# Moving small work between ACT, VectorE and a PSUM bank in the attention part of a sparse-attention and mixture-of-experts kernel

## The chip, the cores and the metric

The kernel runs on one core of one Trainium2 chip. The metric is the device time of one launch in microseconds. The engines are named as in the profile: PE is TensorE (PEld its weight loads), DVE is VectorE, ACT is ScalarE, POOL is GpSimd, SP is SyncE, which issues most of the DMAs.

## What is computed

Attention over 8 batches, 8 heads, 576 positions and 64 channels a head, with two masks of stride 32: heads 0 to 3 look at the last 32 positions, heads 4 to 7 at positions with the same remainder modulo 32. Its output, 512 numbers a position, goes into a gated layer of 8 experts that picks one expert for each position:

```python
scores = scale * np.matmul(q, k.transpose(0, 1, 3, 2))
scores = np.where(masks[None, :, :, :], scores, -1000000000.0)
attn = softmax(scores)                       # over keys
x = (attn @ v) as (B, S, H * D)
...
logits = np.einsum('bsd,de->bse', x, w_gate)
local_gate = sigmoid(x @ w_local)
for b in range(B):
    prev_e = -1
    for s in range(S):
        fresh_e = int(np.argmax(logits[b, s]))
        e = fresh_e if s == 0 or local_gate[b, s] < 0.5 or prev_e < 0 else prev_e
        prev_e = e
        h = np.maximum(x[b, s] @ w1[e], 0.0)
        out[b, s] = softmax(logits[b, s])[e] * (h @ w2[e])
```

## The kernel before

**Two parts.** The first part (`attention`, 0 to about 164 us) computes attention, writes the rows x to memory (`xd`), computes logits and gates, and makes the list of rows for the first expert's first tiles. The second part (`Experts.run`) takes the experts in turn: rows are gathered by an indirect DMA, turned, multiplied by w1, passed through relu, multiplied by w2 and scattered to the output. Pairs of row tiles are multiplied with seven products of half matrices in place of eight, for which sums of the weights (`Weights.sums`, L729) are needed.

**Steps.** The first part is written out by hand, without a scheduler: each engine runs its instructions in the order in which the loop over `n` (L450) issues them. There are 32 pairs of heads, (batch, pair), four a batch, and step n works on several of them at once, as a pipeline:

- it loads operands for pair n + 4, and in steps 5 to 12 a piece of the first expert's weights (SP);
- it computes scores and exponentials of pair n (PE, then ACT; a mask on DVE for the first two pairs of a batch), in two units;
- it stores rows of pair n - 2 if a half batch is complete (`store_x`, POOL for batches 0 and 1, SP after them);
- it turns the rows of pair n - 2 (`turn_x`, L322: PE transposes into PSUM at L330, ACT copies to `xT` at L334);
- it multiplies the exponentials of pair n - 1 by the values (`values`, L288) and divides by the sums (`norm`, L301 and L302 on DVE), unit by unit;
- then, in this order: two pieces of the weight sums (L732 on DVE, in steps 10 to 17), the gates of a batch (`gates`, L372), the stores of probabilities (`store_p`, L411, POOL), the logits of a batch (`logits`, L343), and last what `also[n]` holds.

**Logits and gates.** With `last` the last pair of batch b, logits(b) is in step last + 2 = 4b + 5: steps 5, 9, 13, ... Its products (L354) go to the bank pair of `psT`; the products of the four blocks of channels land on four groups of 32 partitions, and a second product (L382, in `gates`) adds the four groups with a matrix of ones (`fold`). Between the two stands a copy from PSUM to `lT` in four parts: 504 columns and 72 columns of 64 partitions, twice, the second time with the columns in another order. Batches 1, 3 and 5 are twins (`TWINS`, L63) of the batch before: their logits are added to the same `lT` by DVE (L366), and the gates of both are computed together. So gates run for batches 0 and 1 in step 10, 2 and 3 in step 18, 4 and 5 in step 26, 6 in step 30, 7 in step 34. `gates` reads its product four times on DVE (L388, L391, L394, L396) and then works in SBUF.

**PSUM.** Three pools hold 8 banks: `psS` (scores, two buffers of two banks), `psT` (one buffer of two banks: turned rows, logits, and all that asks for `bank()`, L420), `psV` (two buffers of one bank: value products, one for each unit, and the gates). A buffer is given out in turn; its first writer waits until the readers of its last use are done.

**The first gather.** Steps 19 to 29 compute the list of rows (`router.steps` and `router.table`, put into `also`); its last function, `numbers` (L660), runs in step 29, and the index that the gather uses is written at L665. `moe.gather` (L763, L765 on POOL) fetches two tiles of rows, `moe.scale` (L771 on ACT) uses them in step 31.

Of the kernel before, what the change touches and what calls it, by code (L numbers as in the profile page):

```python
# [8 lines left out]
F32 = mybir.dt.float32  # L9
# [9 lines left out]
P = 128  # L19
B, H, S, DH = 8, 8, 576, 64  # L20
# [6 lines left out]
V1 = DH + 1  # L27
# [44 lines left out]
def spread(ap, shape):  # L72

    dims = list("abcd"[:len(shape) - 1])
    left = " ".join(dims[:-1] + [f"({dims[-1]} o)"])
    right = " ".join(dims + ["o"])
    return ap.rearrange(f"{left} -> {right}", o=1).to_broadcast(shape)
# [7 lines left out]
def across(ap, shape):  # L85

    return ap.rearrange("a (o b) -> a o b", o=1).to_broadcast(shape)
# [60 lines left out]
def attention(ctx, tc, qkl, qks, vl, vs, wg, xd, ident, router, moe):  # L148
# [11 lines left out]
    psV = ctx.enter_context(tc.tile_pool(name="psV", bufs=2, space=PSUM))  # L160
# [3 lines left out]
    def load(b, pair):  # L164
        local = pair < PAIRS // 2
        src = qkl if local else qks
        t = inp.tile([P, qkl.shape[-1]], F32, name="qk")
        st["qk", b, pair] = t
        nc.sync.dma_start(out=t[:, 0:src.shape[-1]], in_=src[b, pair % 2])
        if pair % 2 == (b == 0 and local):  # L170
            shape = [LK, LT, 4, V1] if local else [GK, GT, 4, V1]
            t = vals.tile(shape, F32, name="vl" if local else "vs")
            nc.sync.dma_start(out=t, in_=(vl if local else vs)[b])
            st["v", b, local] = t
# [6 lines left out]
    def busy(n):  # L181
        for _ in range(n):
            ps = psV.tile([P, 512], F32, name="vps")
            nc.tensor.matmul(ps, lhsT=warm[:, 0:P], rhs=warm, start=True, stop=True)
# [28 lines left out]
    for n, c in blocks:  # L213

        i, div = consts.tile([GK, 1], I32, name=f"row{n}"), consts.tile([GK, 1], F32, name=f"div{n}")
# [55 lines left out]
    def mask(u):  # L271
        if u.local:
            ev = u.e[:, :, 0:3 * LQ]
            m = maskL[:, 3 * u.g:3 * u.g + 3].rearrange("p a x -> p (a x)")
            nc.vector.tensor_tensor(ev, ev, m.rearrange("p (o x) -> p o x", o=1).to_broadcast([LK, 2, 3 * LQ]),
                                    op=Alu.mult)
# [66 lines left out]
    def logits(b):  # L343
        xT = st["xT", b]
        n = GK * (GT - 1)
        both = ((0, slice(0, n)), (1, slice(n, S)))
        final = b == B - 1

        second = b in TWINS
        w = slice(0, 32) if second else slice(16, 48)  # L350

        ps = [psS.tile([P, 2, 512], F32, name="sps") for _ in range(2)] if final else [psT.tile([P, 2, 512], F32, name="tps")] * 2
        for kk, a, c in [(kk, *x) for kk in range(DK) for x in both] if final else [(kk, *x) for x in both for kk in range(DK)]:
            nc.tensor.matmul(ps[kk // 2][32 * kk:32 * kk + 32, a, 0:c.stop - c.start], lhsT=wgs[:, kk, w], rhs=xT[:, kk, c],  # L354
                             start=True, stop=True, skip_group_check=True)
        if not second:
            st["lT", b] = small.tile([P, S], F32, name="lT")
        lT = st["lT", b] = st["lT", TWINS.get(b, b)]
        o = lT[64:].rearrange("p (y c) -> p y c", c=STRIDE)
        parts = [(lT[0:64, 0:n], ps[0][0:64, 0, 0:n]), (lT[0:64, n:], ps[0][0:64, 1, 0:GL]),  # L360
                 (o[:, :, 0:GC * (GT - 1)].rearrange("p y (j c) -> p j y c", c=GC),
                  ps[1][64:, 0, 0:n].rearrange("p (j y c) -> p j y c", j=GT - 1, c=GC)),
                 (o[:, :, GC * (GT - 1):], ps[1][64:, 1, 0:GL].rearrange("p (y c) -> p y c", c=GR))]
        for i, (to, of) in enumerate(parts):
            if second:
                nc.vector.tensor_tensor(to, of, to, op=Alu.add)  # L366
            elif i == (1 if final else 2) or i == 0:
                nc.scalar.copy(out=to, in_=of)
            else:
                nc.vector.tensor_copy(to, of)  # L370

    def gates(b):  # L372

        b0 = TWINS.get(b, b)
        n = b - b0 + 1
        ps = psV.tile([P, 2, 3, V1], F32, name="vps").rearrange("p a i e -> p (a i e)")
        lt = ps[:, 0:CH * n * (E + 1)].rearrange("p (t b e) -> p t b e", b=n, e=E + 1)
        to = fold.rearrange("p (b x) -> p b x", b=2)[:, 0:n, 0:E + 1]
        for t in range(CH):
            m = min(P, S - t * P)  # L380
            for o in range(0, P, m):
                nc.tensor.matmul(lt[o:o + m, t], lhsT=st["lT", b][:, t * P:t * P + m], rhs=to,  # L382
                                 start=(t == 0), stop=True, skip_group_check=True)
        lg = lt[:, :, :, 0:E]
        one, shape = [P, CH, n], [P, CH, n, E]
        f = lambda name, shape: small.tile(shape, F32, name=f"{name}{n}")
        mx = f("gmx", one)
        nc.vector.tensor_reduce(mx, lg, axis=AX.X, op=Alu.max)  # L388
        mxb = spread(mx, shape)
        ex = f("ex", shape)  # L390
        nc.vector.tensor_tensor(ex, lg, mxb, op=Alu.subtract)  # L391

        eq = f("eq", shape)
        nc.vector.tensor_tensor(eq, lg, mxb, op=Alu.is_equal)  # L394
        fr = f("fr", one)
        nc.vector.scalar_tensor_tensor(fr, lt[:, :, :, E], FRESH, spread(start, one), Alu.is_le, Alu.max)  # L396
        nc.scalar.activation(ex, ex, Act.Exp)
        flat = eq.rearrange("p t b e -> p (t b) e")
        nc.vector.tensor_tensor(flat, flat, across(down, [P, CH * n, E]), op=Alu.mult)
        code = f("code", one)  # L400
        nc.vector.tensor_reduce(code, eq, axis=AX.X, op=Alu.max)
        nc.vector.tensor_tensor(code, spread(pos8, one), code, op=Alu.subtract)

        nc.vector.tensor_tensor(codes[:, :, b0:b + 1], spread(code, shape), spread(fr, shape), op=Alu.mult)
        sm = f("gsm", one)
        nc.vector.tensor_reduce(sm, ex, axis=AX.X, op=Alu.add)
        nc.vector.tensor_scalar(sm, sm, 1e-9, None, Alu.add)
        nc.vector.reciprocal(out=sm, in_=sm)
        nc.vector.tensor_tensor(probs[:, :, b0:b + 1, 0:E], ex, spread(sm, shape), op=Alu.mult)
# [10 lines left out]
    def bank():  # L420
        return psT.tile([P, 8, P], F32, name="tps").rearrange("p a x -> p (a x)")
# [10 lines left out]
    also = {n: [] for n in range(len(units) + 3)}  # L432
# [7 lines left out]
    m = n  # L440
# [2 lines left out]
    early = router.table(0, bank, rooms)  # L443
    for i, do in enumerate(early):
        also[m + i].append(do)
    also[m + 5].append(lambda: moe.gather(moe.first))
    also[len(units) - 1] += [lambda: moe.scale(moe.first)]

    steps = []
    for n in range(len(units) + 3):  # L450
        if n < len(units):
            if n + ahead < len(order):
                load(*order[n + ahead])
            if 5 <= n < 13:
                moe.W[0].load(nc, moe.w1, moe.w2, 0, n - 5)
            if n == 10:
                steps = moe.W[0].sums(nc.vector)
            for u in units[n]:
                scores(u)
                mask(u)  # L460
        if 0 <= n - 2 < len(units) and order[n - 2][1] % 2 == 1:
            store_x(units[n - 2][1])
        if 0 <= n - 2 < len(units) and n != len(units):
            turn_x(*order[n - 2])
        if 0 <= n - 1 < len(units):
            for u in units[n - 1]:
                values(u)
                norm(u)
        if n == len(units):
            turn_x(*order[n - 2])  # L470
            moe.turn(moe.first, spare, 0)
        elif n == len(units) + 1:
            busy(FILL)
        for do in steps[:2]:
            do()
            steps.remove(do)
        for b in range(B):
            last = PAIRS * b + PAIRS - 1
            if n == last + 3 and b + 1 not in TWINS:
                gates(b)  # L480
            if n == last + 4 and b < B - 1 and b + 1 not in TWINS:
                for both in {TWINS.get(b, b), b}:
                    store_p(both)
            if n == last + 2:
                logits(b)
        if n == len(units) + 1:
            moe.turn(moe.first, bank, 1)
            busy(2)
            moe.row_sums(moe.first)
        for do in also[n]:  # L490
            do()
# [1056 lines left out]
```

## Time and profile before

| what | value |
|---|---|
| median of 3 runs | 684.21 us (683.5 to 684.27) |
| the profiled execution | 684.04 us |
| its span, first to last instruction | 682.3 us |
| mean granted clock of PE | 0.994 |
| PE busy | 662.7 us (97%) |
| PE busy in 0 to 164 us | 157.78 us |
| DVE, ACT, POOL busy in the span | 355.5, 194.2, 117.5 us |

The page gives busy time per engine, the granted clock of PE in 40 slices, and the chain of work that ended last. The list of waits says which engine stood idle before which line, until which line on which engine ended: "PE tps L330 <- DVE lT L366: 1.2, 2, 0.9" is 1.2 us in total in 2 places, 0.9 the longest. A line of the timeline has the start in us from the span's start, the duration of the group in us, engine, line, operation, output <- inputs, shape, count, and in brackets the idle time before it with what ended it. A line of the stretches has the stretch and its length, busy time and count for PE, PEld, DVE, ACT and POOL, the granted clock, the share of the DMA engines and GB/s.

### The profile page before, as it was taken

The page shows a single profiled execution, that of the slowest core. Times are in us where ns is not written, and L with a number is a line of the kernel's source. Part 1 is how long each engine was busy: PE and PEld are TensorE (multiplying, and loading weights), DVE is VectorE, ACT ScalarE, POOL GpSimd, SP SyncE. Part 2 cuts the span into 40 slices and gives each one's busy share as a digit, 9 for nine tenths or more (in the row PEclk, how much of TensorE's full clock was granted, in tenths as well). Part 3 has the DMA queues.
Part 4 walks back from the last instruction along what each step waited for, and adds up shares of the span by engine and source line. Part 5 has one row for each costly group of instructions (what it writes and reads, how often), then busy time and mean ns, then how long its engine had stood idle before and what let it go on. Part 6 is the DMA issues. An engine that isn't in the chain of part 4 may idle for free.

```text
span 682.3 us, 14753 instructions
## 1 busy us (share of the span) xinstructions
PE 662.7 (97%) x6020; PEld 570.5 (84%) x6020; DVE 355.5 (52%) x791; ACT 194.2 (28%) x356; POOL 117.5 (17%) x144
## 2 busy tenths in 40 slices
PE   9999999999999999999999999999999999999994
PEld 6888788777998999589979998997799899699493
DVE  6567867846894448026523664651256556522131
ACT  3545445343322221312222222121222232221220
POOL 3431010112021023012011202302111112121001
PEclk9999999989999999999999999999999999999998
DMA  9999877744410182081145217111712622021001
GB/s 324 405 373 331 283 276 276 258 117 140 177 60 35 35 291 69 24 290 36 48 150 174 64 46 268 52 32 40 259 40 65 238 71 73 34 56 42 18 9 37
DMA packets 35801, 95.84 MB, mean 140 GB/s; under 512 B 4790, under 2 KB 11702, under 8 KB 35628
## 3 DMA queue, kind: packets, MB, share of 16 engines
q1 hardware_dynamic: 27164, 71.41, 29.7%
q0 software_dynamic: 7936, 22.38, 10.4%
q8 instruction: 66, 1.08, 0.7%
q14 instruction: 107, 0.88, 0.4%
q10 hardware_dynamic: 528, 0.10, 0.1%
HBM read 74.69 MB, written 19.69 MB: 138 GB/s over the span
## 4 chain that ended last, share of the span: by engine, by line
PE 57%; issue 1%; DVE 1%; DMA 1%; ACT 0%; POOL 0%; POOLq 0%; ACTq 0%
PE lps L835 22%; PE mps L871 21%; PE mps L937 4%; PE lps L926 3%; PE mps L967 2%; PE lps L947 2%; PE xps L778 2%; DMA x<-xd,gi 1%; PE lps L957 0%; DVE h L958 0%; ACT y L973 0%; POOL out_dram L791 0%; DVE wt L732 0%; DVE y L823 0%; ACT x L771 0%
## 5 line engine op out<-in xcount | busy, mean ns | idle before, releaser
L791 POOL DMA_INDIRECT out_dram<-y,tab x40 | 46.1, 1154 | 352.6 <-DVE y L823 248.5
L835 PE MATMUL lps<-tt,ws 128*128 128x128 f32 x768 | 91.8, 275 | 0.6 <-issue 0.6
L835 PEld LDWEIGHTS lps<-tt,ws 128*128 128x128 f32 x768 | 88.6, 192 | 1.0 <-issue 0.8
L871 PE MATMUL mps<-wt,k 128*128 128x256 f32 x384 | 85.7, 380 | 0.0
L871 PEld LDWEIGHTS mps<-wt,k 128*128 128x128 f32 x384 | 72.8, 190 | 9.9
L835 PE MATMUL lps<-xt,w1t 128*128 128x128 f32 x512 | 63.2, 277 | 3.0 <-ACT y L973 1.9
L835 PEld LDWEIGHTS lps<-xt,w1t 128*128 128x128 f32 x512 | 60.4, 192 | 6.5 <-ACT y L973 3.7
L823 DVE TENSOR_TENSOR h<-lps,u 128x512 f32<-128x512 f32 x48 | 33.1, 690 | 57.5 <-PE lps L835 55.8
L871 PE MATMUL mps<-w2t,h 128*128 128x256 f32 x256 | 60.5, 379 | 0.0
L268 ACT ACTIVATE e<-sps 128x576 f32<-128x576 f32 (+1 forms) x64 | 41.5, 650 | 54.3 <-PE sps L264 53.3
L765 POOL DMA_INDIRECT x<-xd,gi x40 | 41.1, 1027 | 82.4 <-PE lps L835 26.3
L871 PEld LDWEIGHTS mps<-w2t,h 128*128 128x128 f32 x256 | 47.4, 190 | 5.8
L264 PE MATMUL sps<-qk 64*128 64x96 f32 (+2 forms) x704 | 51.2, 282 | 0.5 <-issue 0.4
L264 PEld LDWEIGHTS sps<-qk 64*128 64x128 f32 (+2 forms) x704 | 43.0, 185 | 8.8 <-issue 7.4
L822 ACT ACTIVATE h<-h 128x512 f32<-128x512 f32 x48 | 30.2, 630 | 70.1 <-DVE h L823 65.9
L823 DVE TENSOR_TENSOR u<-lps,p 128x512 f32<-128x512 f32 x16 | 11.0, 691 | 54.0 <-PE lps L835 33.1
L822 ACT ACTIVATE h<-lps 128x512 f32<-128x512 f32 (+1 forms) x28 | 15.6, 564 | 82.0 <-PE lps L835 65.8
L771 ACT ACTIVATE x<-x 128x512 f32<-128x512 f32 (+1 forms) x40 | 27.1, 717 | 35.3 <-DMA x<-xd,gi 21.3
L779 ACT COPY xt<-xps 128x512 f32<-128x512 f32 (+1 forms) x38 | 20.3, 565 | 48.8 <-PE xps L778 48.8
L835 PE MATMUL lps<-tt,w1t 128*128 128x128 f32 x256 | 31.3, 275 | 0.0
L835 PE MATMUL lps<-xt,ws 128*128 128x128 f32 x256 | 31.3, 275 | 0.0
L871 PE MATMUL mps<-w2t,k 128*128 128x256 f32 x128 | 30.4, 380 | 0.0
(233 smaller groups left out, 960.4 us busy)
## 6 DMA issues: line engine op xcount, KB each, us to landing
w1t<-in_w_dram SPq DMA_DIRECT2D x7, 2048.0 KB
w2t<-in_w_dram SPq DMA_DIRECT2D x7, 2048.0 KB
qk<-in_qkl_dram SPq DMA_DIRECT2D x16, 592.0 KB
qk<-in_qks_dram SPq DMA_DIRECT2D x16, 576.0 KB
vl<-in_vf_dram SPq DMA_DIRECT2D x8, 780.0 KB
vs<-in_vg_dram SPq DMA_DIRECT2D x8, 639.8 KB
xd<-xl SPq DMA_DIRECT2D x12, 288.0 KB
xd<-xs SPq DMA_DIRECT2D x48, 63.0 KB
```

The source lines that it names most:

```text
L264: nc.tensor.matmul(ps[0:m, h, c:c + w], lhsT=t[r, S + j * width:S + j * width + m], rhs=t[r, j * width:j * width + w], start=(u.local and ...
L268: nc.scalar.activation(e[0:kb, :, 0:n], ps[0:kb, :, 0:n], Act.Exp, bias=0.0, scale=1.0 / DH ** 0.5)
L765: self.nc.gpsimd.indirect_dma_start(out=r.x[0:r.m, i], out_offset=None, in_=self.xd[0:r.rows], in_offset=bass.IndirectOffsetOnAxis(ap=r.gi ...
L771: self.nc.scalar.activation(r.x[0:r.m, i, 0:D], r.x[0:r.m, i, 0:D], Act.Copy, scale=r.gate[i][0:r.m])
L779: self.nc.scalar.copy(out=r.xt[:, i, :, 0:r.m], in_=ps[:, :, 0:r.m])
L791: s = self.nc.gpsimd.indirect_dma_start(out=self.out, out_offset=bass.IndirectOffsetOnAxis(ap=r.si[i][0:r.m], axis=0), in_=y[0:r.m, i], in ...
L822: relu = lambda o, i: nc.scalar.activation(o, i, Act.Relu)
L823: add = lambda o, i, p: nc.vector.tensor_tensor(o, p, i, op=Alu.add)
L835: nc.tensor.matmul(ps[:, f], lhsT=m[:, kk, f * P:(f + 1) * P], rhs=v[:, kk], start=(start and f == 0 and kk == 0), stop=(kk == 1), skip_gr ...
L871: nc.tensor.matmul(ps[:, 0:256], lhsT=m[:, f], rhs=v[:, f], start=(start and f == 0), stop=(f == 3), skip_group_check=True)
L926: nc.tensor.matmul(ps[:, f], lhsT=w.w1[:, kk, c:c + P], rhs=r.xt[:, 0, kk], start=(f == 0 and kk == 0), stop=(kk == DK - 1), skip_group_ch ...
L937: nc.tensor.matmul(ps, lhsT=h[f // 4][:, f % 4], rhs=w.w2[:, f], start=(f == 0), stop=(f == FK - 1))
```

## The change

Four edits, all in `attention`:

- In `logits`, for all batches that are neither twins nor the last, all four parts of the copy to `lT` are made by ACT. Before, ACT made the first and third and DVE the second and fourth (72 columns each). For the last batch nothing changes.
- In `gates`, the product goes to `bank()`, the bank pair of the turned rows, for all batches but the last. Before, it took a buffer of `psV`. For the last batch it stays in `psV`, with the shape written in another way.
- `moe.gather(moe.first)` is put into `also[m + 6]`, step 30, in place of step 29.
- The two pieces of weight sums of a step are issued after gates, stores and logits of that step, before them until now.

```diff
@@ -364,7 +364,7 @@
         for i, (to, of) in enumerate(parts):
             if second:
                 nc.vector.tensor_tensor(to, of, to, op=Alu.add)
-            elif i == (1 if final else 2) or i == 0:
+            elif i < 2 or not final:
                 nc.scalar.copy(out=to, in_=of)
             else:
                 nc.vector.tensor_copy(to, of)
@@ -373,7 +373,7 @@
 
         b0 = TWINS.get(b, b)
         n = b - b0 + 1
-        ps = psV.tile([P, 2, 3, V1], F32, name="vps").rearrange("p a i e -> p (a i e)")
+        ps = psV.tile([P, 512], F32, name="vps") if b == B - 1 else bank()
         lt = ps[:, 0:CH * n * (E + 1)].rearrange("p (t b e) -> p t b e", b=n, e=E + 1)
         to = fold.rearrange("p (b x) -> p b x", b=2)[:, 0:n, 0:E + 1]
         for t in range(CH):
@@ -443,7 +443,7 @@
     early = router.table(0, bank, rooms)
     for i, do in enumerate(early):
         also[m + i].append(do)
-    also[m + 5].append(lambda: moe.gather(moe.first))
+    also[m + 6].append(lambda: moe.gather(moe.first))
     also[len(units) - 1] += [lambda: moe.scale(moe.first)]
 
     steps = []
@@ -471,9 +471,6 @@
             moe.turn(moe.first, spare, 0)
         elif n == len(units) + 1:
             busy(FILL)
-        for do in steps[:2]:
-            do()
-            steps.remove(do)
         for b in range(B):
             last = PAIRS * b + PAIRS - 1
             if n == last + 3 and b + 1 not in TWINS:
@@ -483,6 +480,9 @@
                     store_p(both)
             if n == last + 2:
                 logits(b)
+        for do in steps[:2]:
+            do()
+            steps.remove(do)
         if n == len(units) + 1:
             moe.turn(moe.first, bank, 1)
             busy(2)
```

The instructions on each engine number the same but for DVE and ACT, where eight copies change sides; POOL and SP run the same instructions in the same order.

## The prediction, made before the changed kernel ran

> **What bounds the kernel now.** I read the page first, then the waits of TensorE over the attention part (0 to 164 us), then the timeline around each wait.
>
> ```profile
> PE 662.7 (97%) x6020; PEld 570.5 (84%) x6020; DVE 355.5 (52%) x791; ACT 194.2 (28%) x356; POOL 117.5 (17%) x144
> PEclk9999999989999999999999999999999999999998
> ...
> PE 57%; issue 1%; DVE 1%; DMA 1%; ACT 0%; POOL 0%; POOLq 0%; ACTq 0%
> ```
>
> TensorE (PE) is the bound: busy 97%, and the chain is PE wherever it was followed. So an edit on ACT or DVE is worth only the holes in PE that it closes. The clock row dips once, in the ninth slice (136 to 153 us). The waits list names the holes before the experts begin:
>
> ```profile
> PE vps L382 <- PE vps L288: 1.5, 1, 1.5
> PE vps L184 <- DVE warm L179: 1.4, 1, 1.4
> PE tps L330 <- DVE lT L366: 1.2, 2, 0.9
> PE vps L382 <- DVE sums L301: 0.8, 3, 0.3
> PE sps L264 <- issue: 0.4, 1, 0.4
> PE tps L330 <- ACT xT L334: 0.4, 1, 0.4
> PE vps L288 <- DVE sums L301: 0.3, 1, 0.3
> ```
>
> Lines 1, 3 and 4 are gates and turned rows, 3.5 us together. The other four hold nothing that is edited. The largest piece of line 3 is in step 17:
>
> ```profile
> 81.57 1.28 DVE L732 TENSOR_TENSOR wt<-w2t,wt 128x512 f32<-128x512 f32 x2
> 82.77 1.66 DVE L366 TENSOR_TENSOR lT<-tps,lT 64x504 f32<-64x504 f32 x4
> 84.58 0.85 PE L330 MATMUL tps<-ident,xl 128*128 128x128 f32 x6 [0.93 <-DVE lT L366]
> ```
>
> Two weight sums stand ahead of the four adds that empty the bank, and the next rows are turned 0.93 us late. Line 1 is in step 30, the gates of batch 6:
>
> ```profile
> 143.51 1.73 PE L288 MATMUL vps<-vl,e 128*64 128x65 f32 x48
> 143.75 1.04 POOL L765 DMA_INDIRECT x<-xd,gi  x1 [11.34 <-PE tps L330]
> 145.80 0.20 DVE L301 RECIPROCAL sums<-vps 128x6 f32<-128x6 f32 x1 [2.73 <-PE vps L288]
> 146.74 1.25 PE L382 MATMUL vps<-fold,lT 128*128 128x9 f32 x12 [1.49 <-PE vps L288]
> ```
>
> The gates take the bank of this step's first unit, so they wait for its norm. That norm began at 145.80, 2.29 us after the first value product, against 0.97 us in an ordinary step (30.44 to 31.41). Why TensorE's signal came 1.3 us late is not shown; the first gather runs at the time. Soon after, the clock falls:
>
> ```profile
> 148.50:152.00 3.50, 3.50 (x26) 2.71 (x25) 1.53 (x10) 1.42 (x3) 1.38 (x2) 0.51 0.66 163
> ```
>
> The third number from the end is the clock: about half for 3.5 us.
>
> [...] so the late norm may be a late product or a late signal, and the trace does not part the two. [...] the copies here alternate (ACT 0.57 and 0.61 us, DVE 0.23 and 0.24 us in step 5), each waiting for the other.
>
> **The change part by part.**
>
> *Logits copied by ACT.* In four steps (5, 13, 21, 29) two DVE copies of 72 columns move to ACT. ACT then runs 0.57 + 0.23 + 0.61 + 0.23 = 1.64 us; 0.23 is ACT's own 128x72 copy (226 ns). From 27.60 that ends at 29.24, where the old relay ended at 29.34. TensorE next needs this bank at 29.64, so the cover is 0.40 us of scores; 0.40 also in steps 21 and 29. The strided 72 columns on ACT are not in the trace: from 0.21 us (the plain one on ACT) to 0.61 (the whole big copy), which costs 0 to 0.2 us a step. I take 0. The next exponential starts at 29.24 in place of 29.09 and its values are used a step later. DVE loses eight copies, 1.8 us, and its waits on ACT: nothing on TensorE.
>
> *Sums behind gates and logits.* Nothing is added; the sums issue no DMA, and the gates' stores on POOL (L414) can only come sooner. In step 17 the adds begin at about 81.66 and end at 83.32; TensorE wants the bank at 84.58 - 0.93 = 83.65. Gain 0.93. The sums run to 84.6, before the next norm (86.32 less 0.93 = 85.39). In step 10 the gates' DVE work goes first; twelve small operations and two sums end at about 54.2, where the next norm begins at 54.47. In step 13 no adds are due. The other piece of line 3 (0.31 at 122.9, step 25) stays: no sums are left by then, DVE is late for the table's work.
>
> *Gates in the bank of turned rows.* This takes away the wait for a norm: 3 x 0.28 = 0.84 in steps 10, 18, 26, and 1.49 in step 30. The gates now wait for ACT's copy of the turned rows: at 47.77 + 0.64 = 48.41 it is done, the gates are wanted at 49.28. New wait: the next step's turn (L330) waits until four DVE operations have read the gates; behind it on TensorE stand the values, and for those the norms wait. The gates' products end at 50.82 and L330 comes 2.1 us later (52.94); the four reads took 0.74 us (51.23 to 51.97), so 1.3 us of slack. I take nothing.
>
> *The clock.* [...] Price: from the first mask product of the scores to the first value product is 147.91 to 152.41 = 4.50 us in step 31, and 126.79 to 129.77 = 2.98 us in step 27, the same work. Gain 1.52. From below: 0, if the late signal only moves to another wait and slows the clock there.
>
> *Gather a step later.* On POOL the order and everything that the gather waits for are the same in both programs: the sources of its index (L665), the stores, the table's products. It moves nothing by itself. But L665 on DVE stood behind the last lT copy (142.41); with that gone it follows the norm of 140.33, so the gather starts about 2 us sooner, near 141.6. SP's queue is unchanged. What a sooner gather does to TensorE the trace shows only in the doubtful place: bounded by 0 and by the 1.3 us of the late signal, I take 0, since a delay there meets exponentials with a step of slack.
>
> Sum: 0.93 + 0.84 + 1.49 + 1.52 = 4.78 us. From 164 us on TensorE's program is the same (busy 155.3 of the next 156 us), and the next expert's weights are asked for at 164.16, as this part ends, so all of it shifts along. The profiled execution took 684.04 us (span 682.3, 1.7 around it), the median is 684.21, 0.17 more: 684.21 - 4.78 = 679.4.
>
> **Rivals.**
>
> *A: the stall is TensorE's own and stays.* The late norm is then a late product; the gates no longer wait, but TensorE loses 1.3 us anyway and perhaps the clock. Gain 0.93 + 0.84 = 1.77, to 682.4; with the clock spared, 1.77 + 1.52 = 3.29, to 680.9. For it: both norms of step 30 are late by the same amount, as if the products themselves were. Against it: the products' starts show no hole until all 48 are issued.
>
> *B: no effect that shows.* The edits do not do what they say where other waits lie under the ones removed: DVE's backlog in step 17, the norm in step 18. The holes come back under other names, to 683.0 to 685.
>
> *C: slower, by the bank of turned rows.* It is one bank pair with one buffer; the gates occupy it from the values to DVE's fourth read. If DVE reaches the gates over 1.3 us late, L330 waits in steps 11, 19, 27 and 31. At 1 us each and two slow windows of 1.5 us that is 7 us, less the 4.8 gained: 686.4. Without a slow window it eats the gain from a lateness of 1.3 + 4.8 / 4 = 2.5 us each time. Against it: in the trace the first read follows the products by 0.4 us even behind two sums, which now stand after it.
>
> **How the numbers follow.** The sum holds: 0.50, at 679.4 (678.8 to 680.3 for its own terms). A: 0.34, 680.9 to 682.4. B: 0.10. C: 0.04. Better than the sum, should step 25's 0.31 and the 0.3 of step 31 close too: 0.02, at 678.8. The range 678.6 to 682.7 takes in the sum, A and the little more; it leaves out about 0.16. Measurement tells about 0.2% (1.4 us) from no change, so faster means under 682.8: 0.86; same 0.10; slower 0.04.
>
> **What would show it.** Right: no wait of L382 on a norm; L330 in step 18 following its scores without a hole; no half-rate window near 148; the first gather near 139 to 142 on the clock of the new run; ACT's four lT copies end before L330. Wrong: a hole at L330 behind gmx, ex, eq or fr (C), or behind ACT's lT copies (the strided copy is dear); a norm still over 2 us behind its first value product in step 29 or 30 with the clock at half (A).

## Result and the profile after

| | before | after |
|---|---|---|
| median | 684.24 us (683.5 to 686.87, 6 runs) | 678.76 us (677.4 to 679.77, 6 runs) |
| profiled execution, its span | 684.04, 682.3 us | 679.77, 678.0 us |
| PE busy | 662.7 us | 661.1 us |

The ratio is 0.9916, with a 95% interval of 0.9896 to 0.9936: 5.7 us less (4.4 to 7.1), or 678.5 us from 684.2. The sum of the prediction, 679.4, lies inside that interval, toward its small end. The ratio is one of means, and one run of before, 686.87, lies 2.6 us above the median of its six: the medians differ by 5.5 us, and without that run the means by 5.3. The profiled execution of after is the slowest of its six, so the two traces differ by 4.3 us only.

The page of after, two of its rows:

```profile
PE 661.1 (97%) x6019; PEld 569.3 (84%) x6020; DVE 353.8 (52%) x783; ACT 195.4 (29%) x364; POOL 118.4 (17%) x144
...
PEclk9999999999999999999999999999999999999998
```

Eight operations have gone from DVE (791 to 783) to ACT (356 to 364), and the dip of the clock in the ninth slice is gone. TensorE's waits from 0 to 164 us:

```profile
PE vps L184 <- DVE warm L179: 1.4, 1, 1.4
PE sps L264 <- issue: 0.8, 1, 0.8
PE vps L288 <- issue: 0.4, 1, 0.4
PE tps L330 <- ACT xT L334: 0.4, 1, 0.4
PE vps L288 <- DVE sums L301: 0.3, 1, 0.3
PE tps L330 <- DVE lT L366: 0.3, 1, 0.3
```

Both waits of L382 are gone, and of the 1.2 us at L330 only the 0.3 of step 25 is left, as forecast. Two lines with "issue" (nothing that the profile shows) are new or larger. Step 17, in the timelines of DVE and of PE:

```profile
82.03 1.65 DVE L366 TENSOR_TENSOR lT<-tps,lT 64x504 f32<-64x504 f32 x4
83.71 1.29 DVE L732 TENSOR_TENSOR wt<-w2t,wt 128x512 f32<-128x512 f32 x2
...
84.02 0.87 PE L330 MATMUL tps<-ident,xl 128*128 128x128 f32 x6
```

The adds stand ahead of the sums now and end at 83.68, and the turned rows follow their scores without a hole. Step 30, in the timelines of ACT, POOL, DVE and PE:

```profile
139.51 1.42 ACT L368 COPY lT<-tps 64x504 f32<-64x504 f32 x4 [1.99 <-PE tps L354]
140.39 1.04 POOL L765 DMA_INDIRECT x<-xd,gi  x1 [9.14 <-PE tps L354]
142.35 1.03 PE L288 MATMUL vps<-vl,e 128*64 128x65 f32 x27
143.79 0.84 PE L288 MATMUL vps<-vl,e 128*64 128x65 f32 x21 [0.41 <-issue]
144.10 0.20 DVE L301 RECIPROCAL sums<-vps 128x6 f32<-128x6 f32 x1 [4.39 <-PE vps L288]
144.56 1.28 PE L382 MATMUL tps<-fold,lT 128*128 128x9 f32 x12
```

ACT's four copies take 1.42 us and end at 140.93, ahead of the turned rows (141.55). The gather starts at 140.39. The first norm is late here too: 1.75 us after the first value product (before 2.29, in an ordinary step 0.97). The gates don't care: they follow the values directly. But the values themselves stop behind the 27th of their 48 products; the list shows 0.41 us of it. The norm waits for the first unit's 24 products, which had started on time.

### The profile page after: what moved, and what is told of

Read it like the earlier page. It is cut to its first block, busy times and chain, and to the rows that moved or that the text cites. A ratio compares the mean times of both kernels' runs of the same rounds, so it can differ in the third digit from the quotient of the medians.

```text
span 678.0 us, 14758 instructions
## 1 busy us (share of the span) xinstructions
PE 661.1 (97%) x6019; PEld 569.3 (84%) x6020; DVE 353.8 (52%) x783; ACT 195.4 (29%) x364; POOL 118.4 (17%) x144
## 4 chain that ended last, share of the span: by engine, by line
PE 57%; DMA 1%; issue 1%; DVE 1%; ACT 0%; POOL 0%; POOLq 0%; ACTq 0%
PE lps L835 22%; PE mps L871 21%; PE mps L937 4%; PE mps L967 2%; PE lps L947 2%; PE lps L926 2%; PE xps L778 2%; DMA x<-xd,gi 1%; PE lps L957 0%; POOL out_dram L791 0%; DVE h L958 0%; ACT y L973 0%; ACT x L771 0%; DVE y L823 0%; DVE wt L732 0%
```

## Experiments

All times are the ratio of a kernel to the kernel before on the same chip, turned into us. The kernel before is not the same everywhere: its medians were 684.2 in the first comparison, then 680.8 (e1, e2, e3, e5), 681.2 (e4, e6, e7, e8), 681.05 (e9 to e12) and 684.0 (e13), on chips numbered 8, 9, 3 and 12. The number of the first chip is not on record. My expectations of the first four still count from 684.2.

**One part alone: e1, e2, e3.** e1 moves the sums:

```diff
-        for do in steps[:2]:
-            do()
-            steps.remove(do)
         for b in range(B):
...
                 logits(b)
+        for do in steps[:2]:
+            do()
+            steps.remove(do)
```

> The kernel before with one edit alone: the weight sums of a step are issued behind its gates, stores and logits. Theory (the prediction's first term): the 0.93 us hole at the turned rows (L330) of step 18 goes and nothing else, 684.2 - 0.9 = 683.3; the wait of the gates on a value product in step 30 (1.49) and the half-rate window near 148 us stay. Rival 1: other waits lie under it, and the time stays at 684.2. Rival 2: this edit also moves what follows, and brings more than 1.5 us.

e2 moves the gates:

```diff
-        ps = psV.tile([P, 2, 3, V1], F32, name="vps").rearrange("p a i e -> p (a i e)")
+        ps = psV.tile([P, 512], F32, name="vps") if b == B - 1 else bank()
```

> The kernel before with one edit alone: the gates' product goes to the bank of the turned rows for all batches but the last. Theory (late signal, not late product): the three waits of 0.28 on a norm and the 1.49 in step 30 go, and the half-rate window with them: 684.2 - 0.84 - 1.49 - 1.52 = 680.4; the hole at the turned rows of step 18 (0.9) stays. Rival (the stall is TensorE's own): the late norm of step 30 and a hole of about 1 us stay, perhaps with the half-rate window: 681.9 to 683.4.

e3 gives ACT the copies:

```diff
-            elif i == (1 if final else 2) or i == 0:
+            elif i < 2 or not final:
```

> The kernel before with one edit alone: all four copies of the logits are made by ACT. The gather of the first rows then starts some 2 us sooner, since the index on DVE no longer stands behind the last copy. Theory: nothing by itself, 684.2, within 0.5 us; the gates of step 30 still wait for the norm and the half-rate window stays. Rival: the sooner gather takes its late signal with it, away from the norm that the gates wait for; then part of the 1.49 us hole and perhaps the slow window of 1.5 us go with this edit, down to 681.5.

Measured: e1 0.9982 (0.9974 to 0.9990), 1.2 us less (0.7 to 1.8). e2 0.9985 (0.9978 to 0.9991), 1.0 less (0.6 to 1.5). e3 0.9995 (0.9988 to 1.0001), 0.3 less (-0.1 to 0.8). So each part brings its own term within the noise: forecast 0.93 for e1, for e2 four small gate waits in place of three (1.1), about 0 for e3. But the largest two terms were missing altogether: neither e1 nor e3, whose gates still wait for a norm, has a 1.5 us hole or a slow clock before the last microseconds (mean granted clock 0.996 and 0.997), and the kernel before took 680.8 on this chip, 3.4 less than in the first comparison. TensorE's waits in e1:

```profile
PE vps L382 <- DVE sums L301: 1.1, 4, 0.3
...
PE tps L330 <- DVE lT L366: 0.3, 1, 0.3
```

Four gates wait 0.28 each, step 30 among them. e3 alone could have been put down to its sooner gather (142.14); in e1 the gather is where it was before (143.75), so it is not that.

**All but the gates: e5.** The kernel after with the gates back in `psV`.

> The kernel after with the gates' product back in the value bank; sums, copies and gather as in the kernel after. Theory: only the term of the sums remains, 684.2 - 0.9 = 683.3, with the three small waits of the gates (0.28 each), a hole of 1 to 1.5 us before the gates of step 30 and the half-rate window back. Rival (the sooner gather, not the bank, cleared step 30): no half-rate window, the hole of step 30 small, 680 to 681.

Measured 0.9977 (0.9969 to 0.9986), 1.6 less (1.0 to 2.1), at 679.3. It has no half-rate window (mean granted clock 0.995), which the rival wanted, but four waits of 0.28 for the gates, as e1 has. Since e1 shows the same without the sooner gather, the run says nothing for the rival.

**The kernel after elsewhere: e6, and the kernel before elsewhere: e9.** e6 is after with `also[m + 5]` for the gather; the order of instructions is that of after on every engine.

> The kernel after with the first gather called one step earlier again, which is the same order of instructions on every engine: in effect the kernel after, beside the kernel before on this chip. Theory: where the kernel before shows no late signal and no half-rate window in step 30, the gain is the sum of the single waits alone, 0.93 (turned rows of step 18) + 4 x 0.28 (gates) = 2.0 us, a ratio of 0.997. Rival: the gain is that of the first comparison wherever it runs, 5.5 us, a ratio of 0.992.

> The kernel before, unchanged, profiled on another chip. Theory: where its time is near 681, the first norm of step 30 follows its values by about 1 us, the gates of batch 6 wait 0.3 us, and there is no half-rate window before the last microseconds. Rival: the profile shows the 1.5 us wait and the window here too, and the 681 has another reason.

Measured: e6 0.9956 (0.9943 to 0.9969), 3.0 less (2.1 to 3.9), median 678.17; e9 took 681.45. In e9's timelines step 30 is ordinary, with the same instructions as the kernel before:

```profile
144.35 1.62 PE L288 MATMUL vps<-vl,e 128*64 128x65 f32 x48
145.47 0.20 DVE L301 RECIPROCAL sums<-vps 128x6 f32<-128x6 f32 x1 [1.56 <-PE vps L288]
146.41 1.25 PE L382 MATMUL vps<-fold,lT 128*128 128x9 f32 x12 [0.44 <-DVE sums L301]
```

The norm follows the first value product by 1.12 us (2.29 in the first profile), the gates wait 0.44, and the clock is 1.00 from 146.0 to 149.5 and from 149.7 to 153.0 (0.997 over the run). So the change is worth about 3 us there and over 5 in the first comparison, and the end is the same: 678.2 and 678.5. What differs from chip to chip is the kernel before.

**The hole made by hand: e8, e12, e10.** The first norm of step 30 repeats its reciprocal, six times in e8, three in e12, on the kernel before; six times on the kernel after in e10. (L470 in their lines is the inserted reciprocal.)

```diff
                 values(u)
+                if n == 30 and u.g == 0:
+                    for _ in range(6):
+                        nc.vector.reciprocal(out=sums[:, u.n, :, 0:len(spans(u))], in_=u.ps[:, :, 0:len(spans(u)), DH])
                 norm(u)
```

> The kernel before with the hole of its profile made by hand: the first norm of step 30 repeats its reciprocal six times on DVE (6 x 0.2 = 1.2 us), so the gates of batch 6 wait about 0.3 + 1.2 = 1.5 us on TensorE. Theory: TensorE's clock falls to half for one window of about 3.4 us soon after, as in the first profile, and it costs 1.2 + 1.5 = 2.7 us over the kernel before on the same chip. Rival 1: no window follows, +1.2 us. Rival 2: the wait is taken up by a later one, under +0.5 us.

> The kernel before with a smaller hole made by hand: three repeats of the reciprocal, 0.6 us, so the gates of batch 6 wait about 0.9 us. Theory: too little for a half-rate window, +0.6 us over the kernel before on the same chip. Rival: the window comes after 0.9 us as it does after 1.5: +2.1 us.

> The kernel after with the late norm made by hand: the first norm of step 30 repeats its reciprocal six times on DVE (1.2 us), as in the experiment on the kernel before. Theory: the gates do not wait for the norm any more, so neither the hole nor the half-rate window appears, and the time is that of the kernel after, 678.2 to 678.8, at most 0.3 more. Rival: the delay reaches TensorE by another way (the next turned rows wait for the gates' four reads, the next values for the norm): +1.2 us, or +2.7 with a window.

Measured: e8 1.0041 (1.0028 to 1.0054), 2.8 more (1.9 to 3.7). Its timelines, and the stretch with the clock third from the end:

```profile
145.44 1.35 DVE L470 RECIPROCAL sums<-vps 128x6 f32<-128x6 f32 x6 [1.52 <-PE vps L288]
147.75 1.25 PE L382 MATMUL vps<-fold,lT 128*128 128x9 f32 x12 [1.78 <-DVE sums L301]
```

```profile
149.70:153.00 3.30, 3.30 (x24) 2.50 (x21) 1.36 (x8) 1.29 (x3) 1.38 (x2) 0.50 0.58 149
```

This is the picture of the first profile, made by hand on a chip that doesn't show it: hole, then one window at half rate. Against e9, the same program without the repeats, TensorE loses 1.34 us at the gates and 1.51 in the window.

e12 1.0021 (1.0014 to 1.0028), 1.4 more (1.0 to 1.9). Its trace has a hole of 0.98 and the window as well:

```profile
146.09 1.25 PE L382 MATMUL vps<-fold,lT 128*128 128x9 f32 x12 [0.98 <-DVE sums L301]
```

```profile
148.50:151.80 3.30, 3.30 (x22) 2.51 (x22) 0.96 (x6) 1.19 (x3) 1.38 (x2) 0.50 0.55 145
```

So my expectation, that 0.9 us is too little, fell. In this trace, against e9, the hole costs 0.54 and the window 1.51 us, together the rival's 2.1; the runs show 1.4 and spread from 681.2 to 683.8. The mean granted clock of each run is on record and suggests why: it is 0.992 to 0.994 in the four traces with such a window (before, e4, e8, e12) and 0.995 to 0.997 in the eleven without. Of the 18 runs of e12, 12 are at 0.994 or below, of the 22 of the kernel before beside them 3. So about two thirds of the runs of e12 probably had the window. The 0.93 us hole of step 18 and the 0.44 of e9 were followed by none.

e10 0.9957 (0.9944 to 0.9971), 2.9 less (2.0 to 3.8), median 678.37, as without the repeats. The same delay of the norm no longer reaches TensorE:

```profile
143.05 1.34 DVE L470 RECIPROCAL sums<-vps 128x6 f32<-128x6 f32 x6 [3.61 <-PE vps L288]
143.63 1.28 PE L382 MATMUL tps<-fold,lT 128*128 128x9 f32 x12
...
146.27 0.15 DVE L396 SCALAR_TENSOR_TENSOR fr<-tps,start 128x5 f32<-128x5 f32 x1
...
147.02 0.87 PE L330 MATMUL tps<-ident,xl 128*128 128x128 f32 x6
```

The lines are DVE's and PE's, in order of time. The fourth read of the gates ends at 146.42, and the turned rows that wait for it start at 147.02, so 0.6 us of the new wait's slack is left even then. e8 and e10 together show that this delay costs the kernel before 2.8 us and the kernel after nothing; that it is the gates' edit which does this is read from the lines above, since that edit alone was not run with the delay.

**The gather later for good, or gone: e4, e7, e13.** In e4 the list's last function is a step later; in e7 and e13 two plain loads on SP stand for the first gather (after, and before).

```diff
-        also[m + i].append(do)
+        also[m + i + (i == 5)].append(do)
```

```diff
+            if r is self.first:
+                self.nc.sync.dma_start(out=r.x[0:r.m, i], in_=self.xd[i * P:i * P + P])
+                continue
             self.nc.gpsimd.indirect_dma_start(out=r.x[0:r.m, i], out_offset=None, in_=self.xd[0:r.rows],
```

> The kernel after with the last function of the row list, and so the first gather, one step later for good: the index is written in step 30 after the gates' DVE work, the gather starts near 146 in place of 140. Theory: a late signal of TensorE, if there is one, follows the gather (to 146 to 149), and what it costs TensorE stays under 0.7 us; the time is that of the kernel after within 0.7 us. Rival: the late signal stays at 142 to 144, which would part it from the gather.

> The kernel after with the first gather replaced by two plain loads of the first 256 rows, issued by SP[...]; the rows of the first two tiles are then not those of the first expert, a part of the computation left out. Theory: no signal of TensorE is late by over 0.6 us between 138 and 150, and the time is that of the kernel after or up to 0.7 us less. Rival: the signal is late there all the same, so it has another source than the gather.

> The kernel before with the first gather replaced by two plain loads of the first 256 rows on SP's queue; the rows of the first two tiles are then not those of the first expert, a part of the computation left out. Theory: where the kernel before takes 684 (late signal in step 30), the late norm, the 1.5 us hole and the half-rate window go with the gather, 2.7 us less; where it takes 681, nothing changes, within 0.7 us. Rival: where it takes 684, the late norm stays without the gather.

Measured: e4 0.9998 (0.9986 to 1.0009), the whole gain gone, 680.9 against e6's 678.2 on the same chip. Not by a late signal, of which there is none; the gather's data came too late for its user. The gather started at 147.92 in place of 139.29, and in the timelines of ACT and PE one waits after the other:

```profile
151.46 0.72 ACT L771 ACTIVATE x<-x 128x512 f32<-128x512 f32 x1 [3.37 <-DMA x<-xd,gi]
152.24 0.66 PE L778 MATMUL sps<-ident,x 128*128 128x128 f32 x4 [0.88 <-ACT x L771]
152.96 0.72 ACT L771 ACTIVATE x<-x 128x512 f32<-128x512 f32 x1 [0.77 <-DMA x<-xd,gi]
154.32 0.77 PE L330 MATMUL tps<-ident,xs 128*128 128x128 f32 x5 [1.42 <-ACT xT L334]
```

ACT's scaling waits for the rows, the copies of the turned rows stand behind it on ACT, TensorE waits for both, and in this execution a half-rate window follows (clock 0.50 from 155.30 to 158.60). Both of my theories for e4 looked at the wrong thing.

e7 0.9968 (0.9957 to 0.9978), 2.2 less, no late signal. Since e6 on that chip had none either, it tells nothing about the signal. It shows only that the plain loads bring nothing by themselves there (median 678.92, e6 678.17).

e13 ran on a chip where the kernel before takes 684.0: 0.9959 (0.9941 to 0.9977), 2.8 less (1.6 to 4.0), with the instructions on TensorE untouched.

```profile
144.44 0.20 DVE L301 RECIPROCAL sums<-vps 128x6 f32<-128x6 f32 x1 [1.40 <-PE vps L288]
145.37 1.25 PE L382 MATMUL vps<-fold,lT 128*128 128x9 f32 x12 [0.28 <-DVE sums L301]
```

The norm comes 0.97 us after the first value product (143.47), the gates wait 0.28, the clock is 1.00 from 146.0 to 153.0. Set beside the first profile, the two traces of TensorE agree within 0.2 us up to the gates of step 30, are 1.36 apart there and another 1.5 after the next 3.4 us. So on that chip the loss goes with the first gather. That it is the late norm and its window there too is inferred: the kernel before was not profiled on chip 12, but seven of its eight runs have a granted clock of 0.994 or below, and one of e13's five. What about the gather delays the norm is not shown. The plain loads are issued at 144.80, behind the norm, so e13 takes away POOL's work, the indirect access and all transfers at the time of the gather together.

**One hole more: e11.** Five small operations of `where` (L627 to L631) go to step 23, the large one stays.

```diff
             nc.vector.scalar_tensor_tensor(code, hi, float(E), lo, Alu.mult, Alu.add)
+
+        def spots():
             nc.vector.tensor_tensor(at, across(self.jc, [P, n, NT]), spread(code, [P, n, NT]), op=Alu.is_equal)
...
-        also[m + i].append(do)
+        also[m + i - 1].append(do)
```

> The kernel after with five small DVE operations of the row table (L627 to L631, 0.8 us) moved from step 24 to step 23, where DVE stands idle for 1.05 us. Theory: the adds of step 25 end 0.8 us sooner, the hole of 0.31 at the turned rows of step 26 goes, 0.3 us less than the kernel after, which the trace can show and the times hardly. Rival: the mask of step 24 comes late in its place, and the time stays or grows by 0.3.

Measured 0.9957 (0.9943 to 0.9970), 678.2, the same as e10 on that chip. In the trace the hole is gone (PE's timeline: no wait stands at the turned rows), which no time can tell from nothing:

```profile
121.46 0.87 PE L330 MATMUL tps<-ident,xl 128*128 128x128 f32 x6
```

## Why the prediction was right, and where it was not

The direction, the mechanism and each of its places were right; the size was 0.9 us short, and the low end of the range, 678.6, was set just above the 678.5 of the runs. Each term can be read from how far the same matmuls of two traces lie apart in the group before its place and in the group after it:

| step of the sum | predicted | first pair of traces | e9 to e10 |
|---|---|---|---|
| turned rows of step 18 (0.93) | 0.93 | 0.97 | 0.97 |
| gates of steps 10, 18, 26 (3 x 0.28) | 0.84 | 0.97 (0.32 each) | 0.97 (0.32 each) |
| gates of step 30 | 1.49 | 1.64 - 0.66 | 0.48 |
| clock at half rate | 1.52 | 1.51 | 0 |
| sum | 4.78 | 4.43 | 2.42 |

*The holes, each a little too small.* The step that failed is "3 x 0.28 = 0.84 in steps 10, 18, 26, and 1.49 in step 30", with 0.93 before it: I took a hole's listed length for its worth. The list counts from the modelled end of a matmul. Where the gates waited for nothing, they started 0.07 us before that end. The values and gates of step 18, before and after (PE's timelines):

```profile
85.35 1.62 PE L288 MATMUL vps<-vl,e 128*64 128x65 f32 x48
87.25 1.26 PE L382 MATMUL vps<-fold,lT 128*128 128x18 f32 x12 [0.28 <-DVE sums L301]
```

```profile
84.83 1.62 PE L288 MATMUL vps<-vl,e 128*64 128x65 f32 x48
86.38 1.29 PE L382 MATMUL tps<-fold,lT 128*128 128x18 f32 x12
```

In after the values end at 86.45 by the list, and the gates start at 86.38. From values to gates it is 1.90 us before and 1.55 after: 0.35 for a hole of 0.28, of which the gates' own products give back 0.03, so 0.32 stays. The other holes likewise bring 0.04 more than listed: 0.93 brings 0.97, the 0.44 of e9 brings 0.48. At step 30 it is 0.15 more, because the values ran 0.11 us longer there in the first profile (1.73 against 1.62). Measured, the five holes brought 0.04 + 0.13 + 0.15 = 0.32 us more than listed and the window 0.01 less: 4.78 + 0.32 - 0.01 = 5.09. That is the table's sum without the loss of 0.66.

*The clock.* That the half rate would go with the hole was my estimate; the one trace of before showed only their order. For step 30 the runs bear it out: a hole made by hand there (1.78 and 0.98 us) is followed by a window in the traces of e8 and e12, and e9, with 0.44 us, has none. Why a hole is followed by a window is not shown.

*Rival A was partly true.* In the trace of after TensorE itself lost 0.66 us within the values of step 30, beside an ordinary step. I had this rival at the 1.3 us of the late signal, with 680.9 to 682.4; half of it came, in the one execution that was profiled, and it is part of why that was the slowest of six. In e6 the place shows nothing. Whether the late norm was a late product or a late signal is not decided. In neither trace did one of the 24 products that the norm waits for start late; when they ended is not shown, since the profile models the ends.

*The rest, from 5.1 to 5.7 us, is not traced to a cause.* The interval (4.4 to 7.1) holds both, and by the medians the gain is 5.5. Outside the places of the change, the first pair of traces differs by 0.42 us in the first 7 us of TensorE's work (after is later), by 0.34 at an "issue" hole at 60 us (after is later), and by 0.6 net in the experts (after is sooner). The same hole at 60 us measured 0.2 to 0.8 us in fourteen of the fifteen traces, with and without the edits, and nothing in e6. My range "678.8 to 680.3 for its own terms" had no room for this, and the low end took in only another 0.2. About 0.5 us to either side would have held the result.

*Copies on ACT at nothing:* right, e3 0.3 less (-0.1 to 0.8). The four copies took 1.42 us, not 1.64, so the strided 72 columns were not dear. *The new wait of L330 at nothing:* right, and e10 shows 0.6 us of slack left with the norm 1.2 us late. *The gather, about 2 us sooner and worth nothing by itself:* right in time (140.39 where after is 1.2 us ahead, so 141.6 on the clock of before, as forecast), and the 2 us are slack. e4 shows that this slack ends when the gather starts at 148: then it costs 2.7 us.

*Rival B, no effect:* refuted by e1 and e2, in whose traces each closes its own holes and opens none under another name. *Rival C, slower through the bank:* no wait of L330 behind the gates' reads in any trace of the attention part.

*What I could not see in one profile* is that the two largest terms are not there in every execution. With 1.49 - 0.28 = 1.2 for the late norm and 1.5 for the window, 2.7 of the 4.8 us exist only where the norm is late: in the first comparison and, by e13's times, on chip 12. In ten traces from chips 8, 9 and 3 with the gather in its place, the first operation of the norm comes 0.97 to 1.16 us after the first value product, so none is over 0.2 late. There the kernel before seldom has the slow clock: 14 of its 101 runs are at 0.994 or below, none of them profiled. That the first comparison, like the profile, ran where the norm is late was luck: the sum had not worked it out. On the other chips the same sum, made from e9's trace, would have been 0.93 + 0.84 + 0.44 = 2.2, or 2.4 with the overlap, and the measured gain was 3.0 (2.1 to 3.9). Why the norm is late beside a gather in some places and not in others stays open.

## What to carry to other kernels

Look for waits of the bounding engine that hang on a small operation of another engine. Here such a wait, of TensorE for a norm on DVE, took 0.28 to 0.44 us with the norm in time (e1, e9); with the delay of e8 TensorE lost another 1.34 us there and 1.51 in a window of half clock. Taking the dependency away (here by a buffer that was free anyway) made the kernel immune to a delay of 1.2 us (e10, 678.37 us), which is worth more than the holes listed on a chip without it. When you price a removed hole on TensorE, add the overlap of neighbouring matmuls (here 0.04 us a hole), and leave room in the range for places where two executions of one program differ.

## What the runs showed of the hardware

- Half rate came in four traces, once in each before the last microseconds: in the first profile for 3.41 us (148.58 to 151.99) after the hole of 1.49 us before the gates of step 30; in e8 after 1.78 us there and in e12 after 0.98 (clock 0.50 from 149.70 to 153.00 and from 148.50 to 151.80); in e4 after 0.88 and 1.42 us close together (0.50 from 155.30 to 158.60). After the 0.93 us of step 18 in the first profile (clock 1.00 from 5.30 to 148.50) and the 0.44 of e9 it did not come. What decides it is not shown.
- A window at half rate cost 1.5 us of TensorE's work (e8, e12 and the first profile 1.51 each), less than half of the 3.41 that it lasted in the first profile.
- The kernel before took 683.2 to 685.5 us on chip 12 and 679.6 to 682.4 on chips 8, 9 and 3. In the first profile, at 684.0, a norm is late by 1.3 us beside an indirect DMA and a half-rate window follows; in e9, at 681.5, the norm is late by 0.15 and no window follows. That this parts chip 12 from the others is inferred from e13 and the granted clocks.
